# First token tile's transposes in three pieces with own banks, one piece copied by DVE, one zero product instead of five, second tile's transposes held between two V steps

## The chip, the cores and the metric

One core of a Trainium2 chip. The metric is the device time of one execution in microseconds, of which lower is better. Most executions of a kernel agree within 0.3%. Every version is timed beside the kernel before on the same chip, in rounds. Times inside a profile count from the start of that execution's span.

## The reference, cut to what matters

A token block of 2048 x 640 is normalised; then an attention with feature maps (32 heads of 20) and a gated MLP (1536 wide) run on the same normalised tokens, and both are added to the input.

```python
xn = _layernorm(x, axis=-1)
return x + _A_ref(xn, A_wqkv, A_w_phi, A_wo) + _B_ref(xn, B_w1, B_w3, B_w2)
```

What matters here is the beginning. Nothing on TensorE (PE) can start before a tile of 128 tokens is loaded, normalised on DVE and transposed on PE, and the transposed pieces are copied from PSUM to SBUF. The first useful matmuls are V = xn @ wv for the first tiles.

## The kernel before

The kernel has no fixed loop. Twelve generators yield steps ("streams": normalise, transpose, attention, MLP and so on). A scheduler, run while the program is built, keeps a model of each engine's time and takes, again and again, the step that could start first on PE. A change of a tenth of a microsecond in a modelled cost can thus reorder work much later.

The first two tiles, as before (cuts marked):

```python
def keep_warm(n, rep, rate=2400):            # zero products, meant to keep PE's clock up
    for _ in range(rep):
        mm(bank(7, 128 * n), zero[:], ..., True, True, cost=128 * n / rate)

def warm_up():
    keep_warm(4, 8, 1200)
    keep_warm(1, 9, 1200)

def xn_transpose(t, k, c0=0, c1=DC):         # c0:c1 = which 128 columns of 640
    for dc in range(c0, c1):
        tr(PSb[...], x_tok[:, t, 128 * dc:128 * dc + 128])
    ...
    if t < 2:
        copy("ACT", o, src)
    else:
        evac(o, src)                         # ACT or DVE, whichever the model has free

def norms():
    ...
    yield lambda: ln_apply(0, 0, 256)        # first tile, columns 0:256
    done["first"] = 1
    yield lambda: act_rstd(1)
    yield lambda: ln_apply(0, 256, D)        # first tile, the rest
    done["first"], done["ln"] = 2, 1
    yield lambda: ln_sums(2, 0)              # statistics of the third tile, first half
    yield lambda: ln_apply(1)                # second tile
    done["ln"] = 2
    ...

def transposes():
    for c, c0, c1 in ((1, 0, 2), (2, 2, DC)):
        while done["first"] < c:
            yield None
        yield lambda c=c, c0=c0, c1=c1: (xn_transpose(0, banks(1), c0, c1), keep_warm(1, 4 - c))
    done["t"] = 1
    ...

def attention():
    yield warm_up
    ...
        if t == 0:
            for lo, hi in ((0, 2), (2, 4), (4, DC)):   # three V steps of the first tile
                yield lambda lo=lo, hi=hi: v_first(lo, hi)
```

The softmax here doesn't subtract the row's maximum and nothing guards it: scores larger than these inputs give would overflow.

## Time and profile before

| | before |
|---|---|
| median of 3 executions | 266.67 us (266.32 to 266.89) |
| span of the profiled execution | 265.6 us |
| PE busy | 98% of the span |
| first V step / second V step | 6.58 / 7.40 us |
| last matmul | 263.47 us |

In a timeline line the columns are: start and busy time in us, engine, source line (a helper's, the same for nearly all), operation, output<-input by the program's names, shapes, and count; in brackets the idle time before it and what ended it. "PS<-WVK,xnT" are V (and later K) matmuls, "PS<-ident,x_tok" transposes, "PS<-zero" zero products; "BATCH_NORM_STATS2" are a tile's statistics, "TENSOR_SCALAR x_tok" normalises a tile. A group's busy time runs to the modelled end of its last matmul, so neighbours overlap.

### The profile page before, as it was taken

How to read it: one execution, taken by the hardware profiler on the slowest of the kernel's cores; microseconds unless marked ns; L12 is line 12 of the kernel's file. 1: busy time of each engine (PE TensorE's matmuls, PEld its weight loads, DVE VectorE, ACT ScalarE, POOL GpSimd, SP SyncE). 2: the span in 40 equal slices, each digit the busy share in tenths (PEclk: the TensorE clock that was granted, in tenths of full speed). 3: DMA queues.
4: the chain of work that ended last, by engine and by line, in shares of the span. 5: the costliest groups of instructions: out<-in, count | busy, mean ns of one | idle time of the engine just before them, and what ended most of it. 6: DMA issues, size and time to landing. Idle time of an engine off the chain costs nothing.

```text
span 265.6 us, 4673 instructions
## 1 busy us (share of the span) xinstructions
PE 261.2 (98%) x1875; PEld 156.6 (59%) x1898; DVE 184.3 (69%) x314; ACT 105.6 (40%) x225; POOL 96.0 (36%) x107
## 2 busy tenths in 40 slices
PE   8999999999999999999999999999999999999997
PEld 4655545565556746556554666555565657777773
DVE  4568999999869597769779695869695871211112
ACT  5646988799563235143144504054424010000000
POOL 4311587989969030604306070304361300000000
PEclk9999999999999999999999999999999999999999
DMA  7996078823300794374441527231909162231211
GB/s 227 271 309 186 4 160 238 172 52 52 121 2 0 177 252 79 69 93 77 101 81 26 111 52 155 61 70 26 136 6 178 42 139 52 74 95 56 75 50 49
DMA packets 62742, 27.73 MB, mean 104 GB/s; under 512 B 49920, under 2 KB 62720, under 8 KB 62720
## 3 DMA queue, kind: packets, MB, share of 16 engines
q1 hardware_dynamic: 62576, 27.26, 45.1%
q8 instruction: 15, 0.25, 0.4%
q10 hardware_dynamic: 144, 0.16, 0.2%
q14 instruction: 7, 0.06, 0.1%
HBM read 12.81 MB, written 2.62 MB: 58 GB/s over the span
## 4 chain that ended last, share of the span: by engine, by line
PE 95%; DVE 3%; ACT 1%; issue 1%
PE PS L104 95%; DVE S L104 1%; ACT eqt L104 1%; DVE rS L104 0%; DVE o_tok L104 0%; DVE t L104 0%; DVE hT L104 0%; ACT th L104 0%; DVE g_s L104 0%; DVE xres L104 0%; DVE zero L104 0%; DVE warm L104 0%
## 5 line engine op out<-in xcount | busy, mean ns | idle before, releaser
L104 PE MATMUL PS<-xnT,w_s 128*128 128x512 bf16 x462 | 105.1, 379 | 1.1 <-issue 0.2
L104 PEld LDWEIGHTS PS<-xnT,w_s 128*128 128x128 bf16 x480 | 46.1, 98 | 50.4 <-DVE xnT L104 0.3
L104 POOL TENSOR_TENSOR eqt<-eqt,rS 128x600 bf16<-128x600 bf16 (+1 forms) x32 | 41.0, 1306 | 85.9 <-DVE rS L104 85.9
L104 ACT ACTIVATE th<-PS 128x512 f32<-128x512 f32 x48 | 28.6, 596 | 71.9 <-PE PS L104 71.8
L104 PE MATMUL PS<-w_s,hT 128*128 128x320 bf16 (+2 forms) x384 | 54.9, 299 | 0.0
L104 DVE SCALAR_TENSOR_TENSOR t<-th,PS 128x512 bf16<-128x512 f32 x48 | 32.3, 672 | 26.0 <-ACT th L104 26.0
L104 PEld LDWEIGHTS PS<-w_s,hT 128*128 128x128 bf16 x384 | 37.1, 98 | 15.1
L104 PE MATMUL PS<-WVK,xnT 128*128 128x512 bf16 (+3 forms) x256 | 45.2, 329 | 0.2
L104 POOL TENSOR_TENSOR ekt<-ekt,rS 128x640 bf16<-128x640 bf16 x32 | 39.9, 1278 | 7.0 <-DVE rS L104 6.9
L104 DVE TENSOR_TENSOR xres<-PS,xres 128x640 bf16<-128x640 f32 (+2 forms) x17 | 13.4, 786 | 37.9 <-PE PS L104 37.9
L104 PEld LDWEIGHTS PS<-WVK,xnT 128*128 128x128 bf16 x260 | 24.2, 98 | 19.9 <-ACT WVK L104 0.4
L104 ACT ACTIVATE eqt<-PS 128x240 bf16<-128x240 f32 (+1 forms) x96 | 27.2, 347 | 20.8 <-PE PS L104 20.3
L104 DVE SCALAR_TENSOR_TENSOR hT<-t,PS 128x512 bf16<-128x512 bf16 x48 | 33.0, 687 | 1.8 <-DVE t L104 0.2
L104 DVE TENSOR_REDUCE S<-ekt 128x64 f32<-128x1280 bf16 x16 | 23.3, 1455 | 2.7 <-ACT ekt L104 2.7
L104 PE MATMUL PS<-Wqp,xnT 128*128 128x360 bf16 (+1 forms) x160 | 24.3, 299 | 0.0
L104 PE MATMUL PS<-wo_s,oT 128*128 128x320 bf16 (+2 forms) x159 | 24.3, 298 | 0.1
L104 DVE TENSOR_REDUCE S<-eqt 128x66 f32<-128x1320 bf16 x16 | 24.1, 1507 | 0.0
L104 ACT ACTIVATE ekt<-PS 128x640 bf16<-128x640 f32 x32 | 22.3, 702 | 1.3 <-PE PS L104 0.8
L104 PEld LDWEIGHTS PS<-Wqp,xnT 128*128 128x128 bf16 x160 | 15.3, 98 | 7.8
L104 PEld LDWEIGHTS PS<-wo_s,oT 128*128 128x128 bf16 x160 | 15.2, 98 | 6.2
L104 DVE RECIPROCAL rS<-S 128x64 f32<-128x64 f32 (+1 forms) x32 | 17.9, 560 | 1.1
L104 DVE TENSOR_TENSOR o_tok<-PS,g_s 128x360 bf16<-128x360 f32 (+1 forms) x32 | 15.7, 491 | 1.1
(51 smaller groups left out, 127.1 us busy)
## 6 DMA issues: line engine op xcount, KB each, us to landing
w_s<-in_B_w_dram SPq DMA_DIRECT2D x6, 640.0 KB, 6.4
xres<-in_A_x_dram SPq DMA_DIRECT2D x16, 160.0 KB, 2.5
out_dram<-xres SPq DMA_DIRECT2D x15, 160.0 KB, 1.8
x_tok<-in_A_x_dram SPq DMA_DIRECT2D x3, 640.0 KB, 5.1
w_s<-in_B_w_dram SPq DMA_DIRECT2D x1, 1920.0 KB, 9.6
wo_s<-in_A_wo_dram SPq DMA_DIRECT2D x1, 800.0 KB, 5.5
WVK<-in_A_wqkv_dram SPq DMA_DIRECT2D x2, 320.0 KB, 3.9
x_tok<-in_A_x_dram SPq DMA_DIRECT2D x3, 160.0 KB, 3.4
```

Source lines behind the costliest of these rows:

```text
L104: o = _Op(eng, lambda: m(*args, **kw), r, w, cost)
```

## The change

The intent: the first V step waits for ACT's copy of two transposed pieces. If each of the first two pieces has a PSUM bank of its own, ACT can copy the first as soon as it is there while DVE copies the second, and the V step starts sooner. The zero products between the transposes are reduced from five to one, so that they don't stand in the way. A new hold puts DVE's copy ahead of the third tile's statistics, and a new condition keeps the second tile's transposes between the first and the second V step.

```diff
-            copy("ACT", o, src)
+            copy("DVE" if t == 0 and c0 == 1 else "ACT", o, src, 2)
@@ norms
         done["first"], done["ln"] = 2, 1
+        while done["t0"] < 2:
+            yield None
         yield lambda: ln_sums(2, 0)
@@ transposes
-        for c, c0, c1 in ((1, 0, 2), (2, 2, DC)):
+        for c, c0, c1 in ((1, 0, 1), (1, 1, 2), (2, 2, DC)):
             while done["first"] < c:
                 yield None
-            yield lambda c=c, c0=c0, c1=c1: (xn_transpose(0, banks(1), c0, c1), keep_warm(1, 4 - c))
+            yield lambda c=c, c0=c0, c1=c1: (xn_transpose(0, 4 + min(c0, 2), c0, c1),
+                                                   keep_warm(1, int(c0 == 1)))
+            done["t0"] = c1
@@ attention
                 for lo, hi in ((0, 2), (2, 4), (4, DC)):
+                    while lo == 2 and done["t"] < 2:
+                        yield None
                     yield lambda lo=lo, hi=hi: v_first(lo, hi)
```

More of the change, by code (lines that the diff above doesn't have):

```diff
@@ L713, in banks @@
         return min(range(0, 9 - n), key=free_at)
-    done = dict.fromkeys(("w", "ln", "t", "f", "k", "v", "n", "kv", "p", "pn", "pt", "q", "o", "h", "m", "first"), 0)
+    done = dict.fromkeys(("w", "ln", "t", "f", "k", "v", "n", "kv", "p", "pn", "pt", "q", "o", "h", "m", "first", "t0"), 0)
     landed, pace, force = {}, [0], [False]
```

## The prediction

> **What bounds the kernel now.** I read the page first, then the list of waits for PE alone, then the timeline of each engine between 5 and 9 us, which is where the first token tile is made and where the diff changes code.
>
> ```profile
> span 265.6 us, 4673 instructions
> PE 261.2 (98%) x1875; PEld 156.6 (59%) x1898; DVE 184.3 (69%) x314; ACT 105.6 (40%) x225; POOL 96.0 (36%) x107
> ...
> PE 95%; DVE 3%; ACT 1%; issue 1%
> ```
>
> The busy line and the chain of waits agree: PE works for 98% of the span, and 95% of the chain that ended last is PE. PE's own list of waits is nearly empty:
>
> ```profile
> PE PS L104 <- DVE warm L104: 1.1, 1, 1.1
> PE PS L104 <- issue: 0.2, 1, 0.2
> ```
>
> The 1.1 us is the start, before any operand exists. The ends of matmuls are modelled, so I checked this with starts: in the timeline a 512 column matmul follows the last by 0.21 us, a 320 column one by 0.135 us, and from 6.58 us to the end at 263.7 us the starts follow at that pace. The exceptions are some 0.13 us near 11.5 us, 0.1 us at 26.0 us, and about 23 holes of exactly one matmul, which are missing records. So the time is: the moment at which PE's unbroken stream begins, plus a fixed amount of matmul work, plus the last add and store. The change can only gain at the front, because it alters no matmul that counts. This is the front (start, busy time, engine, operation):
>
> ```profile
> 5.63 0.39 PE L104 MATMUL PS<-ident,x_tok 128*128 128x128 bf16 x2
> 5.82 0.53 PE L104 MATMUL PS<-zero 128*128 128x128 bf16 x3
> 6.14 0.49 PE L104 MATMUL PS<-ident,x_tok 128*128 128x128 bf16 x3
> 6.46 0.28 PE L104 MATMUL PS<-zero 128*128 128x128 bf16 x2
> 6.58 0.71 PE L104 MATMUL PS<-WVK,xnT 128*128 128x320 bf16 x4
> 7.12 0.44 PE L104 MATMUL PS<-ident,x_tok 128*128 128x128 bf16 x5
> 7.40 0.84 PE L104 MATMUL PS<-WVK,xnT 128*128 128x320 bf16 x5
> ```
>
> ```profile
> 6.06 0.38 ACT L104 ACTIVATE xnT<-PS 128x256 bf16<-128x256 bf16 x1 [0.88 <-PE PS L104]
> 6.66 0.49 ACT L104 ACTIVATE xnT<-PS 128x384 bf16<-128x384 bf16 x1 [0.22 <-PE PS L104]
> ```
>
> ```profile
> 5.61 0.37 DVE L104 TENSOR_SCALAR x_tok<-x_tok,mv,rstd 128x384 bf16<-128x384 bf16 x1
> 5.90 0.48 DVE L104 BATCH_NORM_STATS2 bst<-x_tok 128x6 f32<-128x320 bf16 x1
> 6.44 0.45 DVE L104 TENSOR_SCALAR x_tok<-x_tok,mv,rstd 128x640 bf16<-128x640 bf16 x1
> ```
>
> The reader is to see one chain: two transposes (5.63), ACT's copy of both (6.06 to 6.44), and the first V step (6.58), 0.14 us after that copy. What PE does between 5.82 and 6.58 is in part zero products, which are no work. Then see the row at 7.12: the second tile's five transposes already stand between the first and the second V step. They need the DVE row at 6.44, the second tile's normalisation, which ends at 6.89.
>
> **What the Trainium skill says.** "TensorE: Matmul & The Clock Gate", Part 1 on the clock gate: the array starts at half its clock and gets all of it after a busy window of about 3.4 us, a window that is not tied to the kernel's start. The trace agrees in kind: zero products before 6.46 us follow each other by 0.107 us, transposes at 7.12 us by 0.056 us. Part 4 of the same page says that transposes don't count as busy for this gate; no run yet shows it. "PSUM — Partial Sum Buffer", the section on bank collisions: two engines must not touch one bank at once, and semaphores should guard by bank. That is why the three pieces get banks of their own: two engines copy at once, while PE writes. "VectorE: DVE Perf Modes", on why PSUM operands drop a tier: a 16 bit copy out of PSUM runs at two elements a cycle at best. The trace agrees:
>
> ```profile
> 9.37 0.36 DVE L104 COPY xnT<-PS 128x384 bf16<-128x384 bf16 x1
> ...
> 11.27 0.29 DVE L104 COPY xnT<-PS 128x256 bf16<-128x256 bf16 x1 [0.84 <-PE PS L104]
> ```
>
> 128 more columns cost 0.07 us, about 1.8 elements per ns.
>
> **The change part by part.** *Pieces.* ACT's copies took 0.38 us for 256 columns and 0.49 for 384, so 128 columns are an estimated 0.28 us. The first transpose (5.63) ends 0.31 us later by its row, at 5.94; ACT began 0.04 us after its transposes before, so the copy runs 5.98 to 6.26. PE began 0.14 us after it, so the first V step can begin at 6.40 and not 6.58: 0.18 us sooner. *DVE's copy of the second piece.* By the two rows above 128 columns are 0.22 us. The second transpose ends at 6.02, so it runs from about 6.07 to 6.29. Only the third V matmul needs it, at about 6.70; it is hidden there. *Zero products.* Five become one. The last three transposes wait for the DVE row that ends at 5.98, and could start at 6.06 in place of 6.14; ACT's second copy moves from 6.66 to about 6.60. This removes what stood in the way of a V step at 6.40, nothing more: zero products fill waits. *Clock.* If the full clock still comes at 6.46, the first V matmul runs 0.06 us at half speed, which loses 0.03 us. The first step of four, 0.54 us, then ends its issue at 6.97, in place of 7.12: 0.15 us sooner.
>
> *What that gain meets.* The statistics of the third tile now wait until DVE's copy is in the queue, so the order on DVE, which the built program confirms, is: normalise piece two (to 5.98), copy (6.07 to 6.29), statistics (0.48 us, overlapping its neighbour by the 0.08 us that these rows show: 6.21 to 6.70), normalise tile two (0.45 us: 6.62 to 7.06). That last one ended at 6.89 before, so it is 0.17 us later. PE's transposes of the second tile begin 0.06 us after it, at 7.12 to 7.14, where they were at 7.12. PE is idle from 6.97 on. Their weight loads, prefetched from 6.99 before, are no longer hidden, for perhaps another 0.05 us. The second V step, which the change forces behind these transposes, then starts at 7.42 to 7.47, where it was 7.40.
>
> *Third part, transposes between the V steps.* In the built order of before they stand there already, so the new condition only holds the order and moves nothing. The front's sum: -0.18 (copy), +0.03 (clock), +0.17 (wait for DVE), +0.03 (weight loads) = +0.05 us. After it the next tile's normalisation is later too (8.66 becomes 8.84), just before PE wants it at about 8.9.
>
> *What moves later.* The program is ordered by a scheduler's own model, so a shift of 0.1 us changes the order from about 65 us on. By the built orders two gate-and-up products leave the stretch before the key-value sum and one of them is put just before it; PE reaches that sum one product (10 matmuls, 2.15 us) earlier, at 81.4 instead of 83.5 us. The number of matmuls is the same, so this is neutral unless PE comes to wait. POOL is the engine to look at:
>
> ```profile
> 72.55 2.37 POOL L104 MEMSET v<- 128x512 bf16 x1
> ...
> 79.23 5.01 POOL L104 TENSOR_TENSOR ekt<-ekt,rS 128x640 bf16<-128x640 bf16 x4 [2.12 <-DVE rS L104]
> ```
>
> In the new order one more pair of key normalisations (2.5 us) precedes that memset. I count from POOL's end of tile 12's pair at 71.88: pair to 74.4, small constants 0.7, memset to 77.4, pair to 79.9, first half of the last pair at 81.15. PE needs that half at its sixteenth matmul of the sum, near 81.9. So it still fits, with 0.7 us to spare where there was 1.0.
>
> Total: 266.67 + 0.05, that is 266.7 us.
>
> **Rivals.** (1) *The gain is kept*: DVE releases the second tile in time. For it: 0.18 us are really free on ACT. Against: DVE is filled without a gap from 5.61 to 7.9 us, and a copy was added in front of the instruction that PE waits for. It would give 266.5. (2) *The clock*: with fewer zero products, and transposes that may not count as busy, the gate opens one window of 3.4 us later. PE then does half the work in it: up to +1.7 us, 268.4. Against: 17 zero products from 1.05 to 5.4 us are untouched, and the full clock came 5.4 us after the first. I give it one in twelve. (3) *A new wait downstream*, at the key-value sum or where an output tile now comes sooner after its queries: up to +1 us. Against: the old order, made by the same model, has no such wait over 250 us, and the slack counted above is positive. (4) *The reshuffle gains*: only the 0.1 us at 26 us and the 0.13 us at 11.5 us could go, and both lie before it.
>
> **Range and chances.** The three runs of before spread by 0.57 us, more than what I predict, so the range is about that spread with room for a late clock or a small wait above: 266.2 to 267.3. For 2% either way the time would have to move 5.3 us. The front has not that much to give, and even a late clock with a new wait is under 3 us. Faster 0.01, same 0.98, slower 0.01.
>
> **What would show each step.** ACT's 128 column copy near 0.28 us and the first V row near 6.40 show the gain; a DVE copy of some 0.22 us ahead of the statistics, the second tile's normalisation ending near 7.06, and transposes of that tile at 7.12 or later after a hole in PE show the gain lost. A second V step at 7.30 or sooner proves me wrong there. Zero or V matmuls at half pace beyond 7 us would show rival 2; a PE wait for POOL's ekt near 82 us, or any other in its list of waits after 12 us, rival 3.

## The result, and the profile after

| | before | after |
|---|---|---|
| first measurement: median, 6 runs each | 266.58 us (266.32 to 267.02) | 266.79 us (266.57 to 267.12) |
| ratio, 95% interval | | 1.0006 (0.9993 to 1.0019) |
| second measurement (after_again below): median, 9 and 5 runs | 266.79 us (266.59 to 267.06) | 266.62 us (266.57 to 266.73) |
| ratio, 95% interval | | 0.9994 (0.9982 to 1.0007) |
| first V step / second V step (first profile) | 6.58 / 7.40 us | 6.36 / 7.43 us |
| second V step to last matmul (first profile) | 256.07 us | 256.08 us |

The time is the same; two measurements fall on either side of 1 and neither interval excludes it. The page of the changed kernel: span, busy time by engine, and the chain of waits by engine.

```profile
span 265.6 us, 4663 instructions
PE 261.2 (98%) x1870; PEld 156.1 (59%) x1894; DVE 183.9 (69%) x314; ACT 106.2 (40%) x226; POOL 95.9 (36%) x107
...
PE 97%; DMA 1%; DVE 1%; issue 1%; POOL 0%
```

PE bounds it as it did. (Matmuls are fewer by the four zero products and one missing record.) PE's list of waits has the same two lines as before, 1.1 us at the start and 0.2 us of issue. The front, on PE, in the changed kernel's timeline:

```profile
5.66 0.40 PE L104 MATMUL PS<-ident,x_tok 128*128 128x128 bf16 x2
5.85 0.31 PE L104 MATMUL PS<-zero 128*128 128x128 bf16 x1
6.07 0.50 PE L104 MATMUL PS<-ident,x_tok 128*128 128x128 bf16 x3
6.36 0.95 PE L104 MATMUL PS<-WVK,xnT 128*128 128x320 bf16 x4
7.15 0.44 PE L104 MATMUL PS<-ident,x_tok 128*128 128x128 bf16 x5
7.43 1.66 PE L104 MATMUL PS<-WVK,xnT 128*128 128x320 bf16 x11
```

The first V step does start 0.22 us sooner (6.36, not 6.58). But its group takes 0.95 us where it took 0.71, and the second tile's transposes start at 7.15, where they started at 7.12. The gain is gone before the second V step. ACT's and DVE's timelines show what was asked of them:

```profile
5.99 0.28 ACT L104 ACTIVATE xnT<-PS 128x128 bf16<-128x128 bf16 x1 [0.76 <-PE PS L104]
6.61 0.49 ACT L104 ACTIVATE xnT<-PS 128x384 bf16<-128x384 bf16 x1 [0.34 <-PE PS L104]
```

```profile
6.09 0.22 DVE L104 COPY xnT<-PS 128x128 bf16<-128x128 bf16 x1
6.23 0.48 DVE L104 BATCH_NORM_STATS2 bst<-x_tok 128x6 f32<-128x320 bf16 x1
6.63 0.43 DVE L104 TENSOR_SCALAR x_tok<-x_tok,mv,rstd 128x640 bf16<-128x640 bf16 x1
```

ACT's small copy takes the predicted 0.28 us, DVE's the predicted 0.22 us. The second tile's normalisation now ends at 7.06 instead of 6.89. And POOL, near the key-value sum, as counted in the prediction (memset ending at 77.4, pairs to 82.1):

```profile
75.03 2.37 POOL L104 MEMSET v<- 128x512 bf16 x1
77.01 5.05 POOL L104 TENSOR_TENSOR ekt<-ekt,rS 128x640 bf16<-128x640 bf16 x4
```

PE has no wait there. Two things stay open after this profile. At 7.15 both caps meet: the first V step's fourth matmul started at 7.02 and occupied PE until 7.15, since by the trace's record of the granted clock all of it came at 6.85 us, and not at 6.46 as in before (the starts of the four are 0.27, 0.25 and 0.14 us apart); and DVE released the transposes at 7.06. Which of them holds the front? And is 256.08 us from there to the end a constant?

### The profile page after: what moved, and what is told of

The parts are those of the page before. It is cut to its first block, busy times and chain, and to the rows that moved or that the text cites. A ratio compares the mean times of both kernels' runs of the same rounds, so it can differ in the third digit from the quotient of the medians.

```text
span 265.6 us, 4663 instructions
## 1 busy us (share of the span) xinstructions
PE 261.2 (98%) x1870; PEld 156.1 (59%) x1894; DVE 183.9 (69%) x314; ACT 106.2 (40%) x226; POOL 95.9 (36%) x107
## 4 chain that ended last, share of the span: by engine, by line
PE 97%; DMA 1%; DVE 1%; issue 1%; POOL 0%
PE PS L104 97%; DMA x_tok<-in_A_x_dram 1%; DVE bst L104 0%; POOL rstd L104 0%; DVE x_tok L104 0%; DVE xres L104 0%; DVE mv L104 0%
```

## The experiments

Theory A: DVE's added copy delays the second tile's normalisation, and that spends the gain. Theory B: the first V step itself runs at half clock, so there was nothing to gain. Theory C came from the first runs: the landing (arrival from memory) of the third tile, whose statistics stand ahead of that normalisation on DVE, holds it anyway. Each kernel was timed beside the kernel before; all gave right results. In "delay" and "warm" an emission is repeated, and in "cold" some are dropped, behind the scheduler's back, so that the order of all else stays. The edits are shown cut to what matters, and the comments in them are not in the kernels.

### norm_first: the second tile's normalisation ahead of the statistics

```diff
-        yield lambda: ln_sums(2, 0)
         yield lambda: ln_apply(1)
         done["ln"] = 2
+        yield lambda: ln_sums(2, 0)
```

> The changed kernel with one pair of DVE instructions swapped: the second tile is normalised straight after DVE's copy of the second piece, and the third tile's statistics come after it. PE's later order stays that of the changed kernel. Theory A (DVE's added copy and the statistics behind it are what hold the second tile's transposes): that normalisation starts when POOL is done, near 6.44 us, and ends near 6.89 instead of 7.06; the transposes start at 6.97 to 7.00, the second V step at 7.26 to 7.30 instead of 7.43, and the time falls by 0.13 to 0.17 us against the changed kernel. Theory B (the first V step itself ran on half a clock until 7.15, so there was nothing to gain): with the clock rising as late as 6.85 us the second V step stays at 7.43; with the clock rising at 6.46 or sooner it comes at 7.27.

Measured: 267.20 us, ratio to before 1.0015 (1.0003 to 1.0027): 0.15% slower, with an interval clear of 1, and against both theories. In its profile the second V step did come early, at 7.12. But the third tile, whose statistics were pushed back, came late. Its normalisation on DVE and what PE met:

```profile
8.62 0.45 DVE L104 TENSOR_SCALAR x_tok<-x_tok,mv,rstd 128x640 bf16<-128x640 bf16 x1 [0.28 <-POOL rstd L104]
```

```profile
9.95 1.40 PE L104 MATMUL PS<-WVK,xnT 128*128 128x320 bf16 x8 [0.22 <-DVE xnT L104]
```

It starts at 8.62, where it started at 8.21 in before and 8.38 in after, and the second V step is followed by 256.59 us to the last matmul instead of 256.08. The wait was moved by one tile and grew: 0.51 us lost for 0.08 to 0.31 us won (7.12 against 7.20 and 7.43 in the changed kernel's two profiles; counted from the start of the first piece's normalisation, as below, the win is 0.03 to 0.17 us). DVE in the front is a queue of three tiles' work, and what is put first delays what is put last. One thing is not parted here: by the trace the scheduler also put five V matmuls ahead of the third tile's transposes (9.29 us, 8.93 in the changed kernel) and let DVE and ACT exchange copies near 9.5 us. With a replayed order this edit was not run, so how much of the loss is that order's stays open.

### stats_first: the statistics ahead of the copy

```diff
-        while done["t0"] < 2:
-            yield None
         yield lambda: ln_sums(2, 0)
+        while done["t0"] < 2:
+            yield None
         yield lambda: ln_apply(1)
```

> The changed kernel with the statistics of the third tile (0.48 us) put ahead of DVE's copy, where before has them; the copy then ends near 6.55 us. Theory A: the first pair of V matmuls starts near 6.36, the second pair waits for the copy until 6.66 to 6.70, the second tile's normalisation ends near 6.92, the second V step starts at 7.28 to 7.33, time lower by about 0.1 us than the changed kernel. Theory B: if the clock rises at 6.85 the second V step stays near 7.43. Later instructions are in another order here, which both theories take to cost nothing (under 0.1 us).

Measured: 268.05 us, ratio 1.0048 (1.0036 to 1.0060), the highest median of all. The front is not to blame (second V step at 7.46): from there to the last matmul it takes 257.45 us. PE waits 0.5 us for ACT at 18 us, and the starts of its matmuls show another 0.5 us of holes at 65 to 67 us. My expectation that another later order costs nothing was wrong here.

### zeros_only: the kernel before with one zero product

```diff
-            yield lambda c=c, c0=c0, c1=c1: (xn_transpose(0, banks(1), c0, c1), keep_warm(1, 4 - c))
+            yield lambda c=c, c0=c0, c1=c1: (xn_transpose(0, banks(1), c0, c1), keep_warm(1, 2 - c))
```

> The kernel before with one zero product in place of five, nothing else; every other instruction is in its old place. Both theories: the V step waits for ACT's copy, not for zero products, so it starts at 6.58 and the second step at 7.40; time within 0.1 us of before. If fewer zero products made the clock rise later (the rival of the prediction), products of the V steps would run at half pace up to 9.9 us and the time would rise by up to 1.7 us.

Measured: 266.82 us, ratio 1.0003 (0.9991 to 1.0015): the same. The four zero products cost and bring nothing that can be seen. Its profiled execution, one of its slowest (267.24 us), showed something else, on DVE and then on PE:

```profile
6.62 0.49 DVE L104 BATCH_NORM_STATS2 bst<-x_tok 128x6 f32<-128x320 bf16 x1 [0.70 <-DMA x_tok<-in_A_x_dram]
```

```profile
7.52 0.45 PE L104 MATMUL PS<-ident,x_tok 128*128 128x128 bf16 x5 [0.48 <-DVE x_tok L104]
```

The statistics wait for the third tile's landing, and the second tile, ready since long, stands behind them in DVE's queue. In before's profile that tile had landed by 5.1 us, and they started at 5.90 without a wait. This is theory C.

### no_cond: the new condition undone

```diff
-                    while lo == 2 and done["t"] < 2:
-                        yield None
                     yield lambda lo=lo, hi=hi: v_first(lo, hi)
```

> The changed kernel without the new condition (its third part undone): the scheduler then puts four matmuls of the second V step ahead of the second tile's transposes. Both theories: these must wait for ACT's copy of the last three pieces, which ended at 7.10 in the changed kernel, so they start at 7.24; the transposes follow at 7.78 instead of 7.15 and the second tile's V steps come 0.3 to 0.5 us after their place. I expect 0.1 to 0.4 us more than the changed kernel; if it is equal or faster, the condition bought nothing.

Measured: 266.80 us, ratio 1.0004 (0.9992 to 1.0016). On PE:

```profile
6.14 1.46 PE L104 MATMUL PS<-WVK,xnT 128*128 128x320 bf16 x8
7.43 0.44 PE L104 MATMUL PS<-ident,x_tok 128*128 128x128 bf16 x5
```

Eight V matmuls in a row, then the transposes, at 7.43 and not at 7.78: here ACT's copy of the last pieces ended at 6.82, not 7.10. In this profile the last matmul starts at 263.42; in the changed kernel's second profile, whose first piece was normalised at nearly the same time (5.16, here 5.14), at 263.28. So the condition may be worth 0.14 us at the low end of what I expected; the times don't resolve it.

### cold, warm, delay: the clock and the zero products

```diff
-        keep_warm(1, 9, 1200)                       # cold: these nine are not emitted
+        keep_warm(1, 9, 1200, drop=True)
```

```diff
-        keep_warm(1, 9, 1200)                       # warm: eleven
+        keep_warm(1, 8, 1200)
+        keep_warm(1, 1, 1200, 3)
-                                                   keep_warm(1, int(c0 == 1)))
+                                                   keep_warm(1, int(c0 == 1), times=2))
```

```diff
-                                                   keep_warm(1, int(c0 == 1)))   # delay: ten
+                                                   keep_warm(1, int(c0 == 1), times=10))
```

> The changed kernel without the nine small zero products just before the first transposes (PE idle from 4.46 to 5.66 us); all else as scheduled. It measures how close the clock gate is to not opening. If the gate wants a nearly full window, [...]V matmuls of 320 columns follow each other by 0.267 us until some 10 us, time +1.2 to +1.7 us. If two thirds of a window are enough, nothing changes: time within 0.1 us of the changed kernel, clock up at 6.4 to 6.9.

> The changed kernel with its holes filled by zero products: eleven instead of nine before the first transposes, two instead of one after the second piece. If the moment of the clock's rise hangs on how busy PE was, it rises sooner than 6.85 us and the first V step is at full pace, its fourth matmul by 6.80; the second V step then still waits for DVE (7.12 at the earliest for the transposes), so theory A says 7.40 to 7.43 and no gain. If the rise only hangs on where a free running window falls, it comes anywhere in 6.4 to 6.9 with or without these, and the time is that of the changed kernel within 0.1 us.

> The changed kernel with ten zero products in place of one between the second piece's transpose and the last three: about 0.95 us of useless PE work in front of the last three transposes (9 times 0.107 us at half clock), unknown to the scheduler, so the order stays. The last transposes move from 6.07 to about 6.85 to 7.0, the first V step to about 7.1 and the second, behind ACT's copy of the last pieces, to about 8.0 instead of 7.43. If PE's stream has no slack after the front, as I read it, the time rises by the same 0.5 to 0.6 us. If shifts in the front are absorbed later, it rises by clearly less than 0.3 us.

Measured: cold 266.57 us median of four, of which one is 268.35 and three are 266.42 to 266.66; ratio 1.0008 (0.9975 to 1.0041). The 268.35 is the profiled one. Its PE:

```profile
6.20 1.27 PE L104 MATMUL PS<-WVK,xnT 128*128 128x320 bf16 x4
7.27 0.74 PE L104 MATMUL PS<-ident,x_tok 128*128 128x128 bf16 x5
7.80 2.70 PE L104 MATMUL PS<-WVK,xnT 128*128 128x320 bf16 x11
```

V matmuls follow each other by 0.267 us, half pace, until 9.94 us. The last matmul starts 1.65 us later than in the changed kernel's second profile (264.93 against 263.28), which is the price of one late window that the prediction's rival 2 gave. So with the nine products gone the gate opened late in one execution of four, to judge by the times (only this one was profiled); in the 50 executions of before, after and zeros_only, whose highest is 267.36, it never cost that much.

Warm: 266.70 us, ratio 1.0007 (0.9988 to 1.0026), the clock up before 5.7 us, second V step at 7.17, where theory A had said 7.40 to 7.43: with the clock up, DVE's copy starts at 5.85 and the second tile's normalisation ends at 6.82, not 7.06. Delay: 266.66 us, ratio 0.9997 (0.9982 to 1.0012). Delay was a miss as an instrument: the clock was up before the ten products, so they took 0.056 us each and ended sooner than I had worked out from half clock. PE in its profile:

```profile
5.80 0.72 PE L104 MATMUL PS<-zero 128*128 128x128 bf16 x10
...
7.35 1.66 PE L104 MATMUL PS<-WVK,xnT 128*128 128x320 bf16 x11
```

With nine more zero products ahead of it the first V step starts at 6.53, later than in both profiles of the changed kernel (6.36 and, below, 6.16), and the second at 7.35, between that kernel's 7.43 and 7.20. So it could not show what a real delay costs; the table below does that.

### act_piece: the second piece copied by ACT

```diff
-            copy("DVE" if t == 0 and c0 == 1 else "ACT", o, src, 2)
+            copy("ACT", o, src, 2)
```

> The changed kernel with the second piece copied by ACT again (three pieces, no DVE copy). ACT copies piece one 5.99 to 6.27 and piece two to about 6.47, so the third V matmul can start at 6.61 and is hidden or nearly; the second tile's normalisation on DVE ends at 6.89 again. Theory A: transposes at 6.97 to 7.1, second V step at 7.27 to 7.35, 0.1 us faster than the changed kernel. Theory B with a clock rising at 6.85: second V step at 7.43 still. The later order differs; expected to cost nothing.

Measured: 268.00 us, ratio 1.0046 (1.0032 to 1.0061), the same loss as stats_first and in the same places. The second V step came at 7.35, at the late end of what theory A said, but from there to the last matmul it takes 257.46 us, not 256.08. In PE's waits, and on ACT at 64.6 us:

```profile
PE PS L104 <- ACT WVK L104: 0.5, 1, 0.5
```

```profile
64.57 0.71 ACT L104 ACTIVATE v<-PS 128x640 bf16<-128x640 f32 x1 [1.91 <-POOL v L104]
```

The second line is the memset that I had worried about: in this order ACT has to wait for it, and around it, at 65 to 67 us, the starts of PE's matmuls show 0.5 us of holes. The edit and its side effect had to be parted.

### after_again, act_replay, stats_replay, act_warm: with the order forced

The sequence of the scheduler's 265 choices was written out from the changed kernel and played back, so that the edit is the only difference; the traces agree (act_replay's engines run the changed kernel's sequence but for the one copy).

```diff
+    PLAN = "030000001110003113..."       # 265 stream numbers, cut here
-            if heads[i] is None:
+            if heads[i] is None or i != int(PLAN[nth[0]], 12):
                 continue
```

act_replay adds act_piece's line, stats_replay stats_first's lines (and one choice swapped), act_warm is act_replay with the fillings of warm. after_again is the changed kernel as it is.

> The changed kernel once more, beside the three below. Its time should be within 0.15% of before, and the stretch from its second V step to its last matmul 256.08 us, as in before, after, and three of the runs so far, whatever the moment at which that step starts (7.1 to 7.9 us have been seen). If that stretch varies by over 0.1 us, the spread of the times is not made in the front.

> The changed kernel with the second piece copied by ACT, this time with the changed kernel's order of work forced on the scheduler, so that this copy is the only difference. Before, the same edit with a free scheduler was 0.46% slower with three new PE waits (0.65 us at 18 us, 0.5 us at 65 us). If those come from the order, as I now think, they are gone and the stretch from the second V step to the end is 256.08 us again. Theory A (DVE's copy holds the second tile): the normalisation of the second tile ends 1.65 us after the first piece's begins, not 1.70 to 1.81, and the second V step comes 0.05 to 0.15 us sooner after it. Theory C (the third tile's landing holds it, since its statistics stand in front on DVE): the statistics start when that tile lands, at 6.1 to 6.6 us, in most executions, and nothing is gained by taking the copy away: time within 0.1% of the changed kernel.

> The changed kernel with the statistics ahead of DVE's copy, with the changed kernel's order forced otherwise. The free version of it was 0.48% slower; if the order did that, this one is within 0.1% of the changed kernel and its stretch from the second V step to the end is 256.08 us. Where the third tile lands after 6.0 us the copy waits behind the statistics and the third V matmul comes at 6.8 instead of 6.4, the second V step at 7.4 to 7.5: no gain by theory C; by theory A 0.1 us sooner than the changed kernel.

> The version I would now think best: second piece on ACT, order forced, and the holes before the transposes filled with zero products so that the clock is less likely to rise late. All theories: the second V step 1.95 to 2.10 us after the first piece's normalisation (2.17 and 2.18 in before and after), stretch to the end 256.08 us, time 0.05 to 0.2 us below before; since single executions spread by 0.5 us or more, I expect the verdict to be the same within 0.1%.

Measured: after_again 266.62 us, 0.9994 (0.9982 to 1.0007); act_replay 266.84 us, 1.0001 (0.9988 to 1.0014); stats_replay 266.86 us, 1.0000 (0.9987 to 1.0014); act_warm 266.66 us, 0.9996 (0.9983 to 1.0008). The stretch from the second V step to the last matmul is 256.07 or 256.08 us in all four. So the 1.4 us of act_piece and stats_first came from the order, not from the edit.

In after_again the clock was up before the first V step, so theory B's cap is away. On PE and DVE:

```profile
6.16 0.72 PE L104 MATMUL PS<-WVK,xnT 128*128 128x320 bf16 x4
6.91 0.45 PE L104 MATMUL PS<-ident,x_tok 128*128 128x128 bf16 x5
```

The first V step is through at 6.71 (its fourth matmul starts at 6.58), and PE idles until 6.91: the second tile's normalisation ended at 6.86. That is the hole that the prediction asked for. But the copy explains little of it. The normalisation also needs rstd of the second tile (one over its standard deviation), which POOL makes. POOL's row, then DVE's, of after_again:

```profile
5.71 0.63 POOL L104 TENSOR_TENSOR rstd<-mv,mhalf 128x1 f32<-128x1 f32 x1 [0.58 <-DVE mv L104]
```

```profile
5.88 0.23 DVE L104 COPY xnT<-PS 128x128 bf16<-128x128 bf16 x1
6.02 0.48 DVE L104 BATCH_NORM_STATS2 bst<-x_tok 128x6 f32<-128x320 bf16 x1
6.42 0.43 DVE L104 TENSOR_SCALAR x_tok<-x_tok,mv,rstd 128x640 bf16<-128x640 bf16 x1
```

POOL is done at 6.34 and DVE starts at 6.42. In before, without a copy, DVE started 0.03 us after POOL (6.41 and 6.44), and in norm_first, with the copy but without the statistics in between, too (6.29 and 6.32). So copy and statistics together account for about 0.05 us of the 0.20 us hole, and the path through POOL for the rest. In the changed kernel's first profile, where at half clock the copy came at 6.09, they account for 0.17 us (6.43 and 6.63), but there PE was busy until 7.15 anyway.

Counted from the start of the first piece's normalisation, the second V step comes 2.17 us later in before, 2.18 in after, 2.04 in after_again and 2.01 in norm_first, which has POOL's bound alone. Nor does an early clock leave before far behind: in zeros_only, which has before's order and had the clock at 4.63 us by the record, the fourth V matmul started at 6.74. With the third tile landed in time, I estimate its second V step by the rule below at max(6.33 + 0.03 + 0.43 + 0.05, 6.74 + 0.135) + 0.28 = 7.15, 1.99 us after its first piece. No run shows that case.

Does taking DVE's copy away gain the 0.05 us? In act_replay the statistics start thus:

```profile
6.25 0.49 DVE L104 BATCH_NORM_STATS2 bst<-x_tok 128x6 f32<-128x320 bf16 x1 [0.39 <-DMA x_tok<-in_A_x_dram]
```

They wait for the third tile's landing, as theory C says, the normalisation ends at 7.09, and the second V step comes at 7.43. In stats_replay the tile landed still later, at 6.62, the copy stood behind it until 7.25, and the second V step came at 7.95, later than the 7.4 to 7.5 that I had expected. In act_warm it landed early: the statistics started at 5.60 without a wait, the normalisation ended at 6.59, and now PE, still at half clock until 6.33, was the later one; second V step at 7.17. That is 2.24 us after the first piece's normalisation, not the expected 1.95 to 2.10.

So theory C holds in some executions only. By the traces (issue plus time to landing) the third tile landed at 5.0 us in after and 5.1 in before, in both well ahead of its statistics (which start at 6.23 and 5.90), but at 6.2 in act_replay and 6.6 in stats_replay and zeros_only.

All profiles whose later order is before's or the changed kernel's, with no V step at half clock after the second, by the start of the second V step. The last column is the measured time of the very execution that was profiled, less that start:

| profile | second V step | time of that execution | difference |
|---|---|---|---|
| warm | 7.17 | 266.57 | 259.40 |
| act_warm | 7.17 | 266.57 | 259.40 |
| after_again | 7.20 | 266.59 | 259.39 |
| delay | 7.35 | 266.74 | 259.39 |
| before | 7.40 | 266.79 | 259.39 |
| after | 7.43 | 266.83 | 259.40 |
| act_replay | 7.43 | 266.84 | 259.41 |
| zeros_only | 7.81 | 267.24 | 259.43 |
| stats_replay | 7.95 | 267.38 | 259.43 |

Nine executions of eight kernels, with 0.8 us of spread in the second V step, and the rest is constant within 0.04 us. The whole spread of these times is made in the first 8 us, and the later order of the changed kernel costs what that of before costs, within 0.04 us. Part of that spread lies ahead of all these edits: the first tile's landing, after which the first piece's normalisation starts at 4.93 us in act_warm and at 5.27 in delay. norm_first is not in the table; there a wait came after the second V step, and its difference is 259.94. (before's 266.79 is a profiled execution beside the three of its median.)

In these profiles the second V step itself follows from two ends: the later of the normalisation's end plus 0.05 us and the fourth V matmul's start plus 0.135 us, plus 0.28 us for the five transposes. For before that is max(6.93, 7.12) + 0.28 = 7.40; after max(7.11, 7.155) + 0.28 = 7.43; after_again max(6.91, 6.715) + 0.28 = 7.19 (7.20 measured); act_replay max(7.14, 6.875) + 0.28 = 7.42 (7.43). The change moves the fourth V matmul. It pays only where that is the later of the two. In the changed kernel's first profile the late clock kept it late; in the second the normalisation was the later.

## Why the prediction was right

The time (266.7 predicted; 266.79 and 266.62 measured) and the range held. By its own steps:

- *PE's stream is one fixed piece after the front.* Right, and shown: 256.08 us from the second V step on in nine profiles.
- *The gain of 0.18 us for the first V step.* 0.22 us in the first profile; copies of 0.28 and 0.22 us as worked out.
- *DVE's copy delays the second tile by 0.17 us, and that spends the gain.* This step had the wrong path. In the first profile the normalisation did end at 7.06 as predicted, but the hole in PE that should have followed was not there: PE was in the first V step until 7.15. In after_again the hole was there, but POOL's rstd made most of it, and copy and statistics together about 0.05 us. And the second V step came at 7.20, inside the "7.30 or sooner" that the prediction had named as proof against this step (0.07 us of that is an earlier first piece). In other executions it was the third tile's landing: in five of the seven profiles with no copy ahead of the statistics, DVE waited for it, by 0.29 to 0.74 us, and taking the copy away (act_replay) won nothing that could be measured. So the gain was spent mostly by bounds that the copy did not make.
- *Weight loads, +0.03 us.* Too much: from the first of the five transposes to the second V step it takes 0.28 us in before and in after, and 0.29 us in after_again, behind the hole.
- *Clock, +0.03 us.* Mis-sized. The rise was taken from one trace as 6.46 us; it came at 6.85 in the first profile of the changed kernel and before 5.7 in the second. In the first the four V matmuls held PE for 0.79 us (6.36 to 7.15) instead of 0.54, that is +0.25 us. The terms of clock and DVE don't add, though; they are two ends of which the later counts, and both lay near 7.1 us. That the sum of +0.05 came out (+0.03 in the first profile) is therefore luck: there the clock, not DVE, spent the gain, and the second profile gave 7.20.
- *Third part moves nothing.* Right against before's order; no_cond shows that without it the scheduler would now leave that order, for a price of some 0.14 us between two profiles, which the times don't resolve.
- *The later order is neutral.* Right for this kernel, with POOL's memset at 77.4 us as counted. That it was a real risk is shown by two neighbours of it, act_piece and stats_first: other orders of the same work cost 1.3 to 1.4 us.
- *A late clock would cost up to 1.7 us.* The one such execution, in cold, cost 1.65 us. The change as it is showed none.

The search for a better version ended without one: act_warm is at 0.9996 of before with 1 inside its interval. What bounds the front in these profiles is when the first and the third tile land, when POOL has the second tile's rstd, and when the clock rises; the change touches none of them.

## What to carry to other kernels

When one engine streams without a gap to the end, find the row at which the stream starts, and ask of a change whether that row moves, and whether what follows still finds its operands (in norm_first the row came sooner and the time got longer). Here an earlier first V step hardly moved the second. A wait removed at the front meets the next-latest condition, so list all of them with their times, and look at more than one profile, since clock and landings move by more than the change. With a scheduler that orders work by modelled costs, replay the old order before blaming an edit: two edits that looked 0.5% slower were neutral.

## What the Trainium skill lacked or had wrong

- "TensorE: Matmul & The Clock Gate", Part 1, gives 0.5 us either way for the moment of the rise. It also says that the window runs free, and that is the better guide: over these profiles the full clock came between 3.72 us (no_cond) and 6.85 us (after), 2.7 to 5.8 us after PE's first product at 1.05 us, and at 9.94 us in cold's profile, where nine zero products were left out.
- The same page, Part 4, says that the full clock does not engage for transposes. Once the gate was open they ran at the full pace like other matmuls: five transposes at 7.15 us in the changed kernel took 0.44 us, a pace of 0.056 us, where those at 6.07 us, before the gate was open, stood 0.08 to 0.11 us apart. Whether they count as busy for the gate no run here shows.
- No page that I read says how much the landing of one load varies between executions when several are queued. The third tile of 160 KB, asked for at 1.7 us, landed at 5.0 us in after and at 6.6 us in zeros_only and stats_replay; in zeros_only, where the second V step waited for it alone, it came at 7.81 us, 0.4 us later than in before.
